# Splitting some projection products so that every four segment steps hold 3072 TensorE instructions

## The chip, the cores and the metric

The kernel runs on one core of a Trainium2 chip. The metric is the device time of one execution in microseconds (us). The kernel before took 1007.62 us, the median of three runs that lie between 1007.40 and 1008.14 us.

## The reference

Two blocks follow each other: a memory-augmented attention that walks through the sequence in segments of 32 rows, and a gated feed-forward block. The walk is a true recurrence: the memory rows that a segment returns are the memory rows of the next one.

```python
S, Dm, H, Dh, M, seg, F = 2048, 640, 32, 128, 8, 32, 1728
mem = mem0                                   # 8 rows
for s in range(S // seg):                    # 64 segments
    h = concat([mem, layernorm(x)[s * seg:(s + 1) * seg]])      # 40 rows x 640
    q, k, v = h @ Wq, h @ Wk, h @ Wv                            # 32 heads of 128
    p = softmax(where(mask, q @ k.T * Dh ** -0.5, -1e9))
    o = (p @ v) @ Wo                                            # 40 rows x 640
    mem = o[:M]
    outs.append(o[M:])
h = x + concat(outs)
out = h + (relu(layernorm(h) @ W_gate) * (layernorm(h) @ W_up)) @ W_down
```

## The kernel before

**Order of the work.** Every operation is recorded by hand, in program order, on its engine. A small dependency solver then adds the semaphore waits. Nothing is rescheduled: TensorE executes its instructions in the order in which the Python code adds them. A loop `for s in range(1, NSEG)` writes out the 63 segment steps after the first one, and the feed-forward block follows, four blocks of 512 rows. There is no loop left in the program; TensorE has one straight stream of about 48,800 instructions (a matmul that brings its own weight load counts as two, LDWEIGHTS and MATMUL).

**A projection on TensorE.** `project` multiplies the 640 columns of the segment's rows with one half (2048 columns) of Wk, Wq or Wv. The 640 contraction rows are five chunks of 128. In each chunk there are four products, one for each group `g` of 32 output partitions: the activations `act[:, c, :]` (128 x 32) are the stationary operand, 512 columns of the weights are the moving operand, and the result goes to partitions 32g to 32g+31 of a PSUM bank. So the 128 x 128 array is used as four column tiles of 32 columns, one for each `g`, and a projection of one half is 20 products of 512 columns. All four products of a chunk use the same activations, but each column tile has to load them for itself.

**Shared weight loads.** The function `again` (L359) emits a matmul without a LDWEIGHTS, for a column tile that still holds the right activations. In the loop of `WAYS`, the first half of a projection walks through the chunks 0 to 4 and the second half through 4 to 0. The second half therefore begins with the chunk that the first ended with, and with `held=True` its first four products go through `again`: four weight loads fewer. The value projection does the same after the query projection. That makes three places in a step, 12 weight loads, that are left out.

**A step on TensorE, in order:** keys, half 0 and half 1 (`project(a, ks, 1, ...)`, banks P2 and P3); the products of the probabilities with V of the step before (`pv_x`, L654); queries, half 0 and half 1 (banks P0 and P1); values of half 0, with the scores (L466) laid between; values of half 1, again with scores; then a denser tail: `pv_mem` (L519), `filler` parts, `wo_split` (L582, 32 products of 320 columns), `wo_pass` (L565, 64 products of 160 columns) and a last `filler(2)`. The memory rows of the next segment come out of L582 and L565 through `to_act_split` on VectorE (L605, L606), and the next step's key projection waits for them.

**What differs between steps.** The filler depends on `s % 4`. In steps with `s % 4` of 2, 3 and 0 it projects the memory rows of four later segments (`extra_units`, products of 512 columns on banks BQ). In steps with `s % 4 == 1` from s = 5 on it is `woe_pass` (L625, products of 320 columns with Wo), of which 28 products stand behind `wo_pass` as the last TensorE work of the step.

Of the kernel before, what the change touches and what calls it, by code (L numbers as in the profile page):

```python
# [163 lines left out]
def build_kernel(nc, A_x, A_mem0, A_Wq, A_Wk, A_Wv, A_Wo, A_seg_len, B_W_gate, B_W_up, B_W_down, out):  # L164
# [7 lines left out]
    DC = D // 128  # L172
# [91 lines left out]
    P0, P1, P2, P3 = 4, 5, 6, 7  # L264
# [97 lines left out]
            stop_tensor_calc=stop, tile_size=(128, 32 if g is not None else 128), tile_position=(0, 32 * (g or 0)),  # L362
            bass_skip_group_check=True, ldweights=False))

    def project(act, akeys, j, halves, banks, chunks=range(5), ends=(0, DC - 1), held=False):
        swap = 1 if j == 2 and akeys[0][0] == "acte" else 0

        def f(pe):
            for c in chunks:
                for n, i in enumerate(halves):  # L370
                    for g in range(4):
                        o = 2048 * i
                        w = (W[:, j, c, o + 512 * (g ^ swap):o + 512 * (g ^ swap) + 512] if j == 2 else
                             W[:, j, c, o:o + 2048].rearrange("p (h e) -> p h e", e=128)[:, :, 32 * g:32 * g + 32])
                        a = (bank(banks[n])[32 * g:32 * g + 32, :], act[:, c, :], w)
                        if n == 0 and not (held and c == chunks[0]):
                            ins = pe.matmul(*a, start=(c == ends[0]), stop=(c == ends[1]), skip_group_check=True)  # L377
                        else:
                            ins = again(pe, *a, c == ends[0], c == ends[1], g)
            return ins  # L380
        add("pe", f, r=list(akeys) + [("W", j, c) for c in chunks], w=[B(b) for b in banks] + [("Wdone", j)])
# [540 lines left out]
    row_stats(xl, ("xl",), n_rows(1))  # L922
    row_scale(xl, ("xl",), n_rows(1), xl, ("xl",))

    WAYS = ((range(DC),), (range(DC - 1, -1, -1), (DC - 1, 0), True))

    for s in range(1, NSEG):
        last = s == NSEG - 1
        par = s % 2
        nb = s // 4 + 1  # L930
        ln = 64 + 128 * nb < S

        e2 = EARLY.index((s + 1) // 4 * 4 - 1) if (s + 1) // 4 * 4 - 1 in EARLY else None
        e2c = EARLY.index(s - 4) if s - 4 in EARLY else None
        more = 64 + 128 * (nb + 1) < S
        units, evac = extra_units(s)
        woe = s % 4 == 1 and 5 <= s < NSEG - 3 or s == NSEG - 2

        def filler(n):
            if units:  # L940
                units(n)
            if woe:
                woe_pass(BQ[0], WPARTS[n])
        if s > 0:
            a, ks = pass_act(s)
            for i in range(2):
                project(a, ks, 1, (i,), ((P2, P3)[i],), *WAYS[i])
                to_tok((P2, P3)[i], i, "act")
                if last and i == 1:
                    load_piece(("Ko", 0), "act")  # L950
                flip(i, Ko, i, [("Ko", i)])
            if s % 4 == 2 and more:
                row_std(n_rows(nb + 1))
                row_scale(xl, ("xl",), n_rows(nb + 1), xl, ("xl",), "pool")
            if s % 4 == 1 and e2 is not None:
                row_std(128)
                row_scale(xt, ("xt",), 128, xt, ("xt",), "pool")
            pv_x(s - 1, 0)
            norm_x(0)
            if s % 4 == 0 and e2 is not None:  # L960
                add_attn(xt[:, :], xt, at, [("xt",), ("at",), ("rx",)], [("xt",)], "pool")
                dma(h_d[128 * e2:128 * e2 + 128, :], xt[:, :], r=[("xt",)], w=[("h_d", e2)])
            if s % 4 == 2:
                merge_v(s, 1)
            if not last:
                for i in range(2):
                    project(a, ks, 0, (i,), ((P0, P1)[i],), *WAYS[i])
                    to_tok((P0, P1)[i], 2 + i, "act")
                    flip(2 + i, Qo, i, [("Qo", i)])
                    if i == 0:  # L970
                        norm_x_late(0)
                        flip_ox(s - 1, (0,))
            else:
                norm_x_late(0)
                flip_ox(s - 1, (0,))
            if s == NSEG - 2:
                dma(xn2T[0][:, :, :], xn2_d[:, :, :], r=[("xn2_d", u) for u in range(4)] + [("Wdone", 0)],
                    w=[("xn2", 0, u) for u in range(4)])
            project(a, ks, 2, (0,), (P2,), range(4), held=not last)
            scores(s, 0, (0, 1))  # L980
            project(a, ks, 2, (0,), (P2,), (4,))
            scores(s, 0, (2, 3))
            if not last:
                exp_mem(s, 0)
                mask_mem(s, 0)
            to_v(P2, Vp, 0, ("Vp",), "act")
            if last:
                load_piece(("Vp", 0), "act")
            if s % 4 == 1 and ln:
                if n_rows(nb) == 128:  # L990
                    flip_rows(chunks_of(at[:, :]), xl, ("xl",), ("at",))
                else:
                    ln1_trans(nb, xl, ("xl",), BQ[1])
                if more:
                    ln1_load(nb + 1, xl, ("xl",))
        if last:
            project(a, ks, 2, (1,), (P3,))
            to_v(P3, Vp, 1, ("Vp",), "act")
            merge_v(s, 0)
            flip_ox(s - 1, (1,))  # L1000
            exp_x(s, 0)
            gate_up(0, 0)
            scores(s, 1)
            exp_x(s, 1)
            load_piece(("g1", 0), "act")
            mask_x(s)
            late_o(s - 1)
            break
        project(a, ks, 2, (1,), (P3,), range(4))
        scores(s, 1, (0, 1))  # L1010
        project(a, ks, 2, (1,), (P3,), (4,))
        scores(s, 1, (2, 3))
        flip_ox(s - 1, (1,))
        if s == NSEG - 2:
            load_piece(("Pm", 0))
        exp_mem(s, 1)
        to_v(P3, Vp, 1, ("Vp",), "act")
        merge_v(s, 0)
        pv_mem(s, 0)
        norm_mem(s, 0)  # L1020
        exp_x(s, 1)
        exp_x(s, 0)
        mask_mem(s, 1)
        flip_mem(s, 0)
        if e2c is not None:
            flip_rows(chunks_of(at[:, :]), xt, ("xt",), ("at",))
        filler(0)
        if s == NSEG - 2:
            load_piece(("om", 0))
        pv_mem(s, 1)  # L1030
        filler(1)
        norm_mem(s, 1)
        flip_mem(s, 1)
        late_q(s + 1, [("oT", par, "m", 1)])
        if s == NSEG - 2:
            p = 1 - place(s + 1)[0]
            add("pool", lambda o, p=p: o.tensor_copy(Qo[:, :, M:32], Qe[p][:, :, M:32]), r=[("Qe", p, i) for i in range(2)],
                w=[("Qo", i) for i in range(2)])
        if s > 0 and not woe and s != NSEG - 3:
            late_o(s - 1)  # L1040
        if s % 4 == 1 and ln:
            n = n_rows(nb)
            if n < 128:
                copy_op("act", chunks_of(at[:, :])[:, :, 0:n], chunks_of(bank_bf(BQ[1])[:, 0:D])[:, :, 0:n], [B(BQ[1])],
                        [("at",)])
            ln1_back(nb, chunks_of(at[:, :]), [("at",)], "pool")
        mask_x(s)
        if e2c is not None:
            dma(xn2_d[:, :, 128 * e2c:128 * e2c + 128], chunks_of(at[:, :]), r=[("at",)], w=[("xn2_d", e2c)])
        if s % 4 == 3 and e2 is not None:  # L1050
            dma(xt[:, :], x_ap[128 * e2:128 * e2 + 128, :], w=[("xt",)])
            load_attn(at, e2, [], ("at",))
        wo_split(par, P1)
        fold_split(P1, "dve" if s % 4 == 1 else "pool")
        wo_pass(par, P3, (1,))
        to_act_split(s + 1, P3)
        if s >= 1:
            rows_split(P3, P1, wtok, ("wtok",))
            store_attn(wtok, ("wtok",), M, 32 * (s - 1), RID)
        filler(2)  # L1060
        if woe:
            for n in ((s - 2, s - 1) if s == NSEG - 2 else (s - 1,)):
                late_o(n)
        if s % 4 == 0 and e2 is not None:
            row_moments(xt, ("xt",), 128)
        if s % 4 == 1 and more:
            row_moments(xl, ("xl",), n_rows(nb + 1))
        if evac:
            evac()
        if woe:  # L1070
            woe_sum(BQ[0])
            woe_store(s // 4 - 1)
        if s == NSEG - 4:
            p, j = place(NSEG - 1)
            add("pool", lambda o, p=p, j=j: o.tensor_copy(act_e[1 - p][:, :, M:32], act_r[p][:, j, :, M:32]),
                r=[("act", p, "x", j), ("act", p, "x")], w=[("acte", 1 - p)])
# [74 lines left out]
    s = NSEG - 1  # L1151
# [131 lines left out]
```

## Time and profile before

| what | value |
|---|---|
| median of three runs | 1007.62 us |
| the profiled execution's own time | 1006.39 us |
| its span from the first to the last instruction | 1004.7 us |
| TensorE busy | 971.1 us (97% of the span), 25153 matmuls |
| TensorE weight loads | 23308, beside the matmuls |
| VectorE, ScalarE, GpSimd busy | 712.9, 524.7, 167.4 us |
| granted TensorE clock | 1.000 |
| instruction transfers of queue q8 | 190 packets, 3.11 MB |

The profiled execution is 1.2 us shorter than the median of the other runs, and 1.7 us of its time lie outside the span. In the rows of groups, a line such as `L377 PE MATMUL ps<-W,act_r 128*32 128x512` names the source line, the engine, the operation, what is written and read, the array tile and the moving operand; behind the bar stand the busy time of the group and the mean duration of one in ns. The duration of a matmul is partly modelled; the distance between starts is what the stream costs. "Issue" as releaser means that the engine was idle and that the profile shows nothing that it waited for. A step of the loop takes about 12 us: the first key products of the steps 5 and 9 start at 105.28 and 153.91 us, 48.6 us for four steps.

### The profile page before, as it was taken

Reading aid. Unit: us, or ns where it says so; the run is one execution under the profiler, and the core shown is the slowest. Engines: PE = TensorE matmul, PEld = TensorE weight load, DVE = VectorE, ACT = ScalarE, POOL = GpSimd, SP = SyncE. Lnnn points to the kernel's source line nnn. Section 1 sums busy time; section 2 is a strip of 40 time slices with the busy share of each in tenths; the row PEclk is TensorE's granted clock in tenths of the full one; section 3 lists DMA queues with packets and bytes.
Section 4 is the critical chain, followed back from the end, with each engine's and each line's share of the span. In section 5 each row is a group of like instructions: output and inputs, shape, how many; then the busy total and the mean of one; then the engine's idle time right before and its main releaser. Section 6 shows DMA issues by size and latency. Waiting matters only on the chain.

```text
span 1004.7 us, 53813 instructions
## 1 busy us (share of the span) xinstructions
PE 971.1 (97%) x25153; PEld 495.7 (49%) x23308; DVE 712.9 (71%) x1863; ACT 524.7 (52%) x1331; POOL 167.4 (17%) x416
## 2 busy tenths in 40 slices
PE   3789999999999999999999999999999999999998
PEld 0245555555555554555555555555555555344443
DVE  2568787878878887888788878787878765445332
ACT  0456566556666666666666666665656643122121
POOL 7020202121302130222022212111110010000000
PEclk9999999999999999999999999999999999999999
DMA  9931212121212111121212131211111158413100
GB/s 373 418 102 28 53 28 55 33 55 50 53 41 54 49 53 47 47 54 47 53 41 63 47 55 40 41 41 38 40 29 40 38 165 251 108 20 92 27 14 26
DMA packets 72421, 73.01 MB, mean 73 GB/s; under 512 B 41632, under 2 KB 59008, under 8 KB 70272
## 3 DMA queue, kind: packets, MB, share of 16 engines
q1 hardware_dynamic: 70064, 68.27, 23.6%
q8 instruction: 190, 3.11, 1.3%
q10 hardware_dynamic: 2128, 1.31, 0.5%
q14 instruction: 39, 0.32, 0.1%
HBM read 37.04 MB, written 6.55 MB: 43 GB/s over the span
## 4 chain that ended last, share of the span: by engine, by line
PE 93%; SPq 3%; DMA 2%; issue 1%; DVE 1%; ACT 0%; POOL 0%; DVEq 0%; ACTq 0%
PE ps L377 43%; PE ps L841 11%; PE ps L359 10%; PE ps L565 7%; PE ps L582 6%; PE ps L625 4%; SPq L324 3%; PE ps L1088 3%; PE ps L466 2%; PE ps L654 2%; DMA Wo<-in_A_Wo_dram 2%; PE ps L519 2%; PE ps L854 0%; PE ps L1100 0%; DVE TBf L605 0%
## 5 line engine op out<-in xcount | busy, mean ns | idle before, releaser
L377 PE MATMUL ps<-W,act_r 128*32 128x512 bf16 x6832 | 447.4, 380 | 3.1 <-DVE act_r L606 1.8
L377 PEld LDWEIGHTS ps<-W,act_r 128*32 128x32 bf16 x6832 | 169.7, 96 | 212.0 <-issue 63.1
L401 ACT ACTIVATE tok<-ps 128x512 bf16<-128x512 f32 x190 | 109.3, 594 | 57.3 <-PE ps L377 48.8
L377 PE MATMUL ps<-W,act_e 128*32 128x512 bf16 x1224 | 120.0, 383 | 8.0 <-DMA W<-in_A_Wv_dram 3.7
L396 DVE STREAM_TRANSPOSE Ko<-tox 128x512 bf16<-128x512 bf16 x128 | 89.8, 703 | 42.7 <-ACT tox L401 41.5
L474 POOL COPY Qo<-Qe 128x256 bf16<-128x256 bf16 x64 | 28.0, 437 | 528.9 <-DVE oT L539 521.0
L401 ACT ACTIVATE tox<-ps 128x512 bf16<-128x512 f32 x134 | 79.6, 598 | 56.5 <-PE ps L377 35.5
L545 DVE STREAM_TRANSPOSE oT<-tox 128x512 bf16<-128x512 bf16 x128 | 89.8, 702 | 0.0
L396 DVE STREAM_TRANSPOSE Qo<-tok 128x512 bf16<-128x512 bf16 x124 | 85.6, 690 | 0.9
L565 PE MATMUL ps<-Wo,oT 128*32 128x160 bf16 x4032 | 82.3, 233 | 2.8 <-DMA Wo<-in_A_Wo_dram 1.7
L359 PE MATMUL ps<-W,act_e 128*32 128x512 bf16 x856 | 84.6, 385 | 0.0
L582 PE MATMUL ps<-Wo,oT 128*32 128x320 bf16 x2016 | 79.8, 299 | 0.5 <-DVE rm L529 0.5
L359 PE MATMUL ps<-W,act_r 128*32 128x512 bf16 x808 | 79.9, 382 | 0.0
L565 PEld LDWEIGHTS ps<-Wo,oT 128*32 128x32 bf16 x4032 | 71.8, 97 | 12.0 <-DMA Wo<-in_A_Wo_dram 2.8
L401 ACT ACTIVATE Vp<-ps 128x512 bf16<-128x512 f32 x127 | 75.2, 592 | 0.5 <-ACT Vp L401 0.5
L869 ACT ACTIVATE g<-ps 128x512 bf16<-128x512 f32 x52 | 30.1, 593 | 79.5 <-PE ps L841 79.5
L595 ACT ACTIVATE SA<-TA 64x40 f32<-64x40 f32 x126 | 29.5, 234 | 77.0 <-DVE TA L593 76.2
L841 PE MATMUL ps<-xn2T,Wu 128*128 128x512 bf16 x259 | 64.5, 379 | 0.1
L870 DVE TENSOR_TENSOR hT<-g,ps 128x512 bf16<-128x512 bf16 x52 | 35.7, 687 | 40.6 <-PE ps L841 38.6
L482 ACT ACTIVATE Pm<-ps 128x64 bf16<-128x64 f32 x126 | 28.1, 223 | 69.2 <-PE ps L466 69.2
L841 PE MATMUL ps<-xn2T,Wg 128*128 128x512 bf16 x247 | 61.8, 379 | 1.3 <-issue 1.0
L582 PEld LDWEIGHTS ps<-Wo,oT 128*32 128x32 bf16 x2016 | 53.9, 97 | 16.0 <-DVE rm L529 1.2
(116 smaller groups left out, 1463.1 us busy)
## 6 DMA issues: line engine op xcount, KB each, us to landing
VM<-Vp SPq DMA_DIRECT2D x126, 65.0 KB
VM<-Vp SPq DMA_DIRECT2D x63, 130.0 KB
W<-in_A_Wk_dram SPq DMA_DIRECT2D x5, 1024.0 KB
W<-in_A_Wq_dram SPq DMA_DIRECT2D x5, 1024.0 KB
W<-in_A_Wv_dram SPq DMA_DIRECT2D x5, 1024.0 KB
Wo<-in_A_Wo_dram SPq DMA_DIRECT2D x8, 640.0 KB
attn_d<-wtok SPq DMA_DIRECT2D x248, 7.5 KB
xt<-in_A_x_dram SPq DMA_DIRECT2D x16, 160.0 KB
```

The costliest lines, as they stand in the source:

```text
L324: add(eng, lambda e: e.dma_start(dst, src), r=r, w=w, dma=True)
L359: return pe.add_instruction(mybir.InstMatmult(name=nc.get_next_instruction_name(), engine=mybir.EngineType.PE, ins=[pe.lower_ap(rhs), pe.l ...
L377: ins = pe.matmul(*a, start=(c == ends[0]), stop=(c == ends[1]), skip_group_check=True)
L396: add("dve", lambda v: v.transpose(dst[:, 16 * i:16 * i + 16, 0:32], tok[t][:, :].rearrange("p (h f) -> p h f", f=32)), r=tok_keys(t), w=keys)
L401: add("act", lambda a: a.activation(dst, src, ACTF.Copy), r=r, w=w)
L545: add("dve", lambda v, kh=kh: v.transpose(ap(oT[p], 160 * kh + M, [[320, 4], [40, 4], [1, 32]]), ap(tox, 128 * kh, [[256, 4], [1, 4], [4, ...
L565: i = pe.matmul(bank(bk)[32 * gg:32 * gg + 32, 0:160], src[:, hb, 0:32], w[:, gg], start=(hb == CH[16 * halves[0]]), stop=(hb == CH[-1]), ...
L582: i = pe.matmul(bank(bk)[32 * q:32 * q + 32, 0:320], src[:, hb, 0:32], w, start=(n == 0), stop=(n == 7), skip_group_check=True)
L625: ins = pe.matmul(bank(bk)[32 * q:32 * q + 32, 0:320], src[:, hb, 0:32], w[:, 2 * (q % 2):2 * (q % 2) + 2], start=(i == 0), stop=(i == 15) ...
L841: ins = pe.matmul(bank(bk), w[:, c, lo:lo + 128], xn2T[par][:, c, :], start=(c == 0), stop=(c == DC - 1))
L870: add("dve", lambda v: v.tensor_tensor(hT[par][:, j, :], g1[gi][:, :], bank(bu), ALU.mult), r=[B(bu), ("g1", gi)], w=[("hT", par, j)])
L1088: i = pe.matmul(*a, start=(j == 0), stop=(j == FC - 1), skip_group_check=True)
```

## The change

`project` gets a parameter `parts`, the number of instructions to add in it. As long as some are left, a product (in a chunk that isn't the first one of the accumulation) is emitted as two of 256 columns, on the same column tile and PSUM bank, one after the other. With two or more left, the second one has its own LDWEIGHTS with the same activations (a split adds two instructions); with one left it goes through `again` (a split adds one). The order of products is otherwise unchanged: tile 0 first half, tile 0 second half, tile 1 first half, and so on.

`fill_of(s)` divides a number of instructions by step: 56, 39, 8 and 52 for `s % 4` of 0, 1, 2 and 3, with 26 in step 1, 29 in step 57 and none from step 61 on. First, up to three of the three `held` places get their four weight loads back (4 instructions each); the rest are splits in the key and query projections, shared over their four halves.

```diff
-    def project(act, akeys, j, halves, banks, chunks=range(5), ends=(0, DC - 1), held=False):
+    def project(act, akeys, j, halves, banks, chunks=range(5), ends=(0, DC - 1), held=False, parts=0):
...
+            left = parts
             for c in chunks:
                 for n, i in enumerate(halves):
                     for g in range(4):
...
                         if n == 0 and not (held and c == chunks[0]):
-                            ins = pe.matmul(*a, start=(c == ends[0]), stop=(c == ends[1]), skip_group_check=True)
+                            k = min(left, 2) if c != ends[0] else 0
+                            left -= k
+                            for q in range(2 if k else 1):
+                                b = a if not k else (a[0][:, 256 * q:256 * q + 256], a[1],
+                                                     w[:, 256 * q:256 * q + 256] if j == 2 else w[:, 8 * q:8 * q + 8])
+                                if q and k == 1:
+                                    ins = again(pe, *b, c == ends[0], c == ends[1], g)
+                                else:
+                                    ins = pe.matmul(*b, start=(c == ends[0]), stop=(c == ends[1]), skip_group_check=True)
                         else:
                             ins = again(pe, *a, c == ends[0], c == ends[1], g)
...
-    WAYS = ((range(DC),), (range(DC - 1, -1, -1), (DC - 1, 0), True))
+    WAYS = ((range(DC), (0, DC - 1)), (range(DC - 1, -1, -1), (DC - 1, 0)))
+    FILL = (56, 39, 8, 52)
+
+    def fill_of(s):
+        n = {1: 26, 57: 29, 61: 0, 62: 0, 63: 0}.get(s, FILL[s % 4])
+        alone = min(n // 4, 3)
+        rest = n - 4 * alone
+        return [k < 3 - alone for k in range(3)], [2 * ((rest // 2 + k) // 4) + (k == 0 and rest % 2) for k in range(4)]
...
+            held, parts = fill_of(s)
             for i in range(2):
-                project(a, ks, 1, (i,), ((P2, P3)[i],), *WAYS[i])
+                project(a, ks, 1, (i,), ((P2, P3)[i],), *WAYS[i], held=i == 1 and held[0], parts=parts[i])
...
-                    project(a, ks, 0, (i,), ((P0, P1)[i],), *WAYS[i])
+                    project(a, ks, 0, (i,), ((P0, P1)[i],), *WAYS[i], held=i == 1 and held[1], parts=parts[2 + i])
...
-            project(a, ks, 2, (0,), (P2,), range(4), held=not last)
+            project(a, ks, 2, (0,), (P2,), range(4), held=not last and held[2])
```

## The prediction

> **What bounds the kernel now.** I read the page from its busy times to the chain that ended last, then the TensorE timeline of some steps, and last the distances between starts, product by product.
>
> ```profile
> span 1004.7 us, 53813 instructions
> ...
> PE 971.1 (97%) x25153; PEld 495.7 (49%) x23308; DVE 712.9 (71%) x1863; ACT 524.7 (52%) x1331; POOL 167.4 (17%) x416
> ...
> q8 instruction: 190, 3.11, 1.3%
> ...
> PE 93%; SPq 3%; DMA 2%; issue 1%; DVE 1%; ACT 0%; POOL 0%; DVEq 0%; ACTq 0%
> ```
>
> TensorE's own stream carries 93% of the chain, so what the change adds or takes there goes into the time nearly one for one. The row q8 is TensorE's instructions on their way in: 3.11 MB over the 48,800 instructions of its stream are 64 bytes each, and 190 packets are 256 instructions each.
>
> The timeline of step 4's end gives the price of products on four column tiles:
>
> ```profile
> 102.13 1.26 PE L582 MATMUL ps<-Wo,oT 128*32 128x320 bf16 x32
> 103.22 1.28 PE L565 MATMUL ps<-Wo,oT 128*32 128x160 bf16 x64
> 104.33 0.39 PE L377 MATMUL ps<-W,act_e 128*32 128x512 bf16 x4
> 104.54 0.39 PE L359 MATMUL ps<-W,act_e 128*32 128x512 bf16 x4
> 104.76 0.39 PE L377 MATMUL ps<-W,act_e 128*32 128x512 bf16 x4
> ```
>
> From start to start, four products (one on each tile) of 512 columns take 0.216 us, of 320 columns 1.09 / 8 = 0.136 us, of 160 columns 1.11 / 16 = 0.069 us. Inside a group of four the starts are 1.7 to 4 ns apart. The tiles work side by side, and each is the length of its moving operand; L377 (with loads) and L359 (without) cost the same, as the loads run under the products before.
>
> What the change is aimed at is seen here:
>
> ```profile
> 115.34 1.07 PE L565 MATMUL ps<-Wo,oT 128*32 128x160 bf16 x51
> 116.65 0.45 PE L565 MATMUL ps<-Wo,oT 128*32 128x160 bf16 x13 [0.24 <-issue]
> ...
> 699.08 0.98 PE L625 MATMUL ps<-Wo,oTe 128*32 128x320 bf16 x21
> 700.71 0.45 PE L625 MATMUL ps<-Wo,oTe 128*32 128x320 bf16 x7 [0.65 <-issue]
> ...
> 807.93 0.31 PE L565 MATMUL ps<-Wo,oT 128*32 128x160 bf16 x6
> 809.06 1.21 PE L565 MATMUL ps<-Wo,oT 128*32 128x160 bf16 x58 [0.82 <-issue]
> ```
>
> TensorE stops in the middle of a run of equal products, and "issue" says that it waits for no semaphore. Counting instructions along the stream, the long stops of this kind stand at one place modulo 256 (193 to 195): the instructions 4547, 10435, 39619 and 46019, for instance, all 195. So they are ends of an instruction block. The q8 packets fit: after TensorE passes a block's end, a packet starts some 1.1 us later, takes 0.9 to 1.6 us, and where there is a stop it ends 1.2 to 1.5 us after the packet's end. From one end to the end of the next stop these are 3.4 to 4.6 us. Where 256 instructions last longer than that, nothing stops; all 512-column regions need over 4 us. Only dense tails stop. Over the steps, ten ends stop visibly, nine of them in steps with `s % 4 == 1` or in steps 32 and 52: about 5.0 us, plus 1.0 us in step 62.
>
> **Alignment.** Four steps have 2917 instructions before, so that ends drift through all places; after, 3072 = 12 x 256, so that they stand at the same twelve places in every cycle from step 3 to step 60. Counted in the changed stream the steps start at 201, 154, 152 and 153 modulo 256 (`s % 4` = 2, 3, 0, 1). With ends at 195 they lie, from a step's start, at 250 and 506; 41, 297, 553; 43, 299, 555; and 42, 298, 554, 810. Eleven are places without a stop in the trace (or close to one). The twelfth, 810 of 816 in `s % 4 == 1`, is three products before the end of L625. As the 39 added instructions stand earlier in the step, it is place 771 of 777 in the old count, and the block before it begins at 515, in L582. These 256 instructions (L582, L565, L625) last 3.28 us in the steps where nothing stops. The nearest ends in the trace are at 750, 756 and 764 (steps 13, 33, 53): all three stop, 0.60, 0.31 and 0.95 us, and TensorE resumes 3.89, 3.43 and 4.12 us after the end before. Against 3.28 us this leaves 0.61, 0.15 and 0.84, mean 0.53, of which 0.06 was spent anyhow waiting for act_r at the next step's first product (0.195 instead of 0.136 us there). So I put 0.47 us on each of the 14 steps 5 to 57: +6.6 us (ends: 0.1 x 14 = 1.4, 0.8 x 14 = 11). Gone are the 5.0 us of drifting stops; the 1.0 us of step 62 stays, for it has the same places but two instructions. Net +1.6 us (-3.6 to +6). The Trainium skill, "Runtime: NRT & Kernel Launch", section Instruction fetch mechanics, also has blocks of 256 instructions, but calls the fetch mostly hidden by the time that each instruction takes to dispatch; by that, alignment is worth 0. The trace disagrees in the tails, with 0.3 to 1 us a stop, and the trace decides.
>
> **Weight loads given back.** 165 places x 4 = 660 loads. A load has a row of 96 ns, but starts while the group of four before still streams (0.216 us); L377 and L359 have the same spacing. Cost 0. Without that cover, as in the first group behind a wait, the next group came 0.226 instead of 0.216 us later: 165 x 0.01 = 1.7 us is the most.
>
> **Splits.** The added matmuls are 828: 22, 14, 0 and 20 for `s % 4` = 0, 1, 2, 3 (15 x 22 + 15 x 20 + 7 + 13 x 14 + 9). A half of 256 columns lasts, between the rows of 160 and 320 columns, 69 + 67 x 96 / 160 = 109 ns. The columns are the same in sum. What counts is the order: both halves are on one tile, next to each other. The second must wait until the tile is free, 109 ns after the first. If later products, for other tiles, do not start ahead of a waiting one, tile 1's first half starts only there, 2 ns after, tile 2's another 111 ns on, and a fully split chunk lets the next one start after 4 x 111 = 444 ns instead of 216: 228 ns for four splits, 57 ns for one. The trace of before never puts two products on one tile in a row in these modes, so that it does not show which holds. It does show all starts in program order (line by line, through 23,900 products), and never a product that passes a waiting one; only weight loads start ahead. The bounds are: tiles go on independently, and a split costs a tile 2 x 69 - 136 = 2 ns, 828 x 2 / 4 = 0.4 us in all; or one behind the other, 828 x 57 ns = 47.2 us. I take the second. The Trainium skill, "TensorE: Matmul & The Clock Gate", Part 3, "The mechanism", speaks against the change in the same way: matmuls start and end in program order, strictly first in, first out; no run here shows it for two on one tile. These 47 us have no cover: no wait of TensorE stands in the key and query stages that could shrink, and the act_r wait stands at the chain's end.
>
> ScalarE and VectorE get the banks later by the same time and have nothing more to do. No DMA is added but nine instruction packets (2302 instructions). The clock is 1.000 and has no idle stretch to fall in.
>
> **Sum.** The profiled execution, 1006.4, + 47.2 + 1.6 + 0.4 (a quarter of the loads' bound) = 1055.6 us; against the median, which is 1.2 us higher, the same within what follows. Own range of this case: 1050 to 1064.
>
> **Rivals.**
> 1. *The tiles run on independently.* For it: the four tiles stream side by side, and weight loads do leave the order. Against it: no product was ever seen to do so. 1006.4 + 0.4 + 1.6 = 1008.4, with the alignment's bounds 1004 to 1013. A measurement of this kernel can tell about 0.2% (2 us) from no change, so this case holds all three signs.
> 2. *Faster: independent tiles and the end at 810 costs nothing.* This decides on the packet: if it lands early enough for TensorE to resume within 3.28 + 0.06 us of the end at 554, no stop is left but step 62's. Step 41 speaks for it: an end at 554, and at the next, 3.47 us later, no stop; step 45 needed less than 3.43. Against it stand steps 13, 33 and 53. 1006.4 + 0.4 - 5.0 = 1001.8 us.
> 3. *A split is dearer.* If the second half's load on the same tile is not hidden, each half pays the 10 ns of the fresh group above: 8 x 10 = 80 ns on a chunk, 20 ns a split, 16.6 us more: 1072 us. Against it: a load lasts 96 ns, a half 109.
>
> That the counts are not what the change says is no case: they are 3072 in the changed stream.
>
> **Chances.** Forecast 0.70; independent tiles 0.15; faster 0.06; dearer 0.09. Slower by over 0.2%: 0.70 + 0.09 + 0.06 of rival 1 = 0.85; within 0.2%: 0.06 of rival 1; faster 0.03 of it and 0.06 = 0.09. The forecast's case and the dearer one's lower end reach to 1066; taking in the upper half of rival 1 (0.09) needs 1007. That leaves out about 0.2.
>
> **What the profile after would show.** Matmuls near 25,981 and loads near 24,782, q8 at 199 packets; a group of 128x256 on the split's line. If the halves queue, the starts of a split chunk are about 0.11 us apart pairwise, and the key and query stages of steps with `s % 4` of 3, 0 and 1 are about 1.1, 1.25 and 0.8 us longer, while steps with `s % 4 == 2` keep 12.0 us: four steps take near 51.9 instead of 48.6 us. If these stages keep their length with the splits in, my forecast is wrong and rival 1 holds. Stops by "issue" should stand in L625 just ahead of the key projection of each step with `s % 4 == 2`, 0.1 to 0.8 us, and nowhere else until step 62; if they are missing there, the alignment pays and my term for it is wrong.

## The result and the profile after

The changed kernel took 1015.63 us (median of five runs), the kernel before 1007.35 us in the same comparison: a ratio of 1.0091 with a 95% interval of 1.0074 to 1.0108. A repeat gave 1.0088 (1.0073 to 1.0104). The change is slower by 9 us; the forecast was slower by 48 us.

A sixth execution of the changed kernel, the one profiled first, took 5677.59 us with its matmuls several times as long, at a granted clock of 1.000, and is left aside; "after" is the profile of the repeat, which took 1015.31 us. Its page:

```profile
span 1013.6 us, 56129 instructions
...
PE 975.6 (96%) x25995; PEld 539.8 (53%) x24782; DVE 716.0 (71%) x1863; ACT 524.7 (52%) x1331; POOL 167.5 (17%) x416
...
q8 instruction: 199, 3.26, 1.4%
```

The span is 8.9 us longer, but TensorE's busy time grew by 4.5 us only (971.1 to 975.6), although it has 828 matmuls more. (The rows differ by 842, because the trace of before lacks the records of 14 matmuls of the feed-forward block.) 199 instruction packets came in, nine more, as counted. The rest is time in which TensorE does nothing. First the query stage of step 4 (a step with 22 splits, 12 of them here), from the timeline:

```profile
97.11 0.42 PE L663 MATMUL ps<-VM,Px 64*32 64x129 bf16 x32
97.46 3.21 PE L386 MATMUL ps<-W,act_r 128*32 128x512 bf16 x68
100.50 0.19 PE L475 MATMUL ps<-Qo,Ko 128*32 128x40 bf16 x4
```

From the first `pv_x` product to the first score it takes 3.39 us with 68 matmuls: the 56 products that stood there before (40 of the queries, 16 of the values) and 12 second halves. Before, the same two starts lie 3.38 us apart:

```profile
95.49 0.42 PE L654 MATMUL ps<-VM,Px 64*32 64x129 bf16 x32
...
98.87 0.19 PE L466 MATMUL ps<-Qo,Ko 128*32 128x40 bf16 x4
```

The splits are nearly free. Now the end of step 53, from the timeline, to be laid beside the stop shown in the prediction at the same step:

```profile
704.68 1.30 PE L574 MATMUL ps<-Wo,oT 128*32 128x160 bf16 x64
705.79 1.00 PE L634 MATMUL ps<-Wo,oTe 128*32 128x320 bf16 x24
707.72 0.32 PE L634 MATMUL ps<-Wo,oTe 128*32 128x320 bf16 x4 [0.93 <-issue]
707.85 0.40 PE L386 MATMUL ps<-W,act_r 128*32 128x512 bf16 x4
```

L634 is the L625 of before. TensorE stops four products before the step's end; the key products behind it start at once when it goes on. And TensorE's waits in sum (line, releaser, us in total, times, longest):

```profile
PE ps L634 <- issue: 5.2, 9, 0.9
...
PE ps L574 <- issue: 1.9, 2, 1.1
```

Before (L565 is the L574 of the changed kernel):

```profile
PE ps L565 <- issue: 1.1, 2, 0.8
PE ps L625 <- issue: 1.0, 2, 0.7
```

This view only counts what lies beyond the modelled end of a matmul; from start to start the stops are longer. Measured so, 12 of the 14 steps with `s % 4 == 1` from 5 to 57 stop at instruction 809 of 816, for 0.25 to 1.09 us, 7.5 us in all. Only the steps 33 and 41 pass. The block ends among the key products, at the places 41 to 43 of a step, stop TensorE as well, in nine steps (3, 9, 11, 21, 23, 27, 40, 52, 57): from the first key product to the first `pv_x` product these take 0.09 to 0.40 us longer than the median of the steps with the same `s % 4`, 1.9 us in sum.

### The profile page after: what moved, and what is told of

It reads as the page before. It is cut to its first block, busy times and chain, and to the rows that moved or that the text cites. A ratio compares the mean times of both kernels' runs of the same rounds, so it can differ in the third digit from the quotient of the medians.

```text
span 5674.8 us, 56129 instructions
## 1 busy us (share of the span) xinstructions
PE 5657.5 (100%) x25995; PEld 1823.6 (32%) x24782; DVE 737.0 (13%) x1863; ACT 532.7 (9%) x1331; POOL 167.6 (3%) x416
## 4 chain that ended last, share of the span: by engine, by line
PE 100%; DMA 0%; DVE 0%; POOL 0%; ACTq 0%; issue 0%; POOLq 0%
PE ps L386 51%; PE ps L850 12%; PE ps L359 9%; PE ps L574 7%; PE ps L591 7%; PE ps L634 4%; PE ps L1105 3%; PE ps L475 2%; PE ps L663 2%; PE ps L528 1%; PE ps L863 0%; PE ps L887 0%; PE ps L1117 0%; DMA wtok<-in_A_mem_dram 0%; ACTq L324 0%
## 5 line engine op out<-in xcount | busy, mean ns | idle before, releaser
L386 PE MATMUL ps<-W,act_r 128*32 128x512 bf16 (+1 forms) x8306 | 2559.0, 1550 | 0.7 <-DVE act_r L615 0.7
L386 PEld LDWEIGHTS ps<-W,act_r 128*32 128x32 bf16 x8306 | 627.8, 291 | 1522.5 <-issue 1516.1
L386 PE MATMUL ps<-W,act_e 128*32 128x512 bf16 x1224 | 520.6, 1701 | 0.4 <-DVE TBf L456 0.4
L574 PE MATMUL ps<-Wo,oT 128*32 128x160 bf16 x4032 | 442.6, 798 | 0.0
L591 PE MATMUL ps<-Wo,oT 128*32 128x320 bf16 x2016 | 440.9, 1211 | 0.0
L574 PEld LDWEIGHTS ps<-Wo,oT 128*32 128x32 bf16 x4032 | 316.7, 321 | 158.2 <-issue 70.0
L359 PE MATMUL ps<-W,act_e 128*32 128x512 bf16 x856 | 365.9, 1708 | 0.0
L850 PE MATMUL ps<-xn2T,Wu 128*128 128x512 bf16 x260 | 364.0, 1708 | 0.0
L850 PE MATMUL ps<-xn2T,Wg 128*128 128x512 bf16 x260 | 361.3, 1698 | 0.0
L1105 PE MATMUL ps<-Wd,hT 128*128 128x320 bf16 (+1 forms) x225 | 259.6, 1197 | 0.0
L591 PEld LDWEIGHTS ps<-Wo,oT 128*32 128x32 bf16 x2016 | 162.8, 323 | 258.5 <-issue 248.6
L359 PE MATMUL ps<-Wd,hT 128*128 128x320 bf16 x195 | 236.2, 1211 | 0.0
L634 PE MATMUL ps<-Wo,oTe 128*32 128x320 bf16 x1024 | 228.7, 1214 | 0.0
L386 PEld LDWEIGHTS ps<-W,act_e 128*32 128x32 bf16 x1224 | 97.9, 319 | 297.9 <-issue 281.5
```

Of the source, the lines that this page charges most:

```text
L359: return pe.add_instruction(mybir.InstMatmult(name=nc.get_next_instruction_name(), engine=mybir.EngineType.PE, ins=[pe.lower_ap(rhs), pe.l ...
L386: ins = pe.matmul(*b, start=(c == ends[0]), stop=(c == ends[1]), skip_group_check=True)
L574: i = pe.matmul(bank(bk)[32 * gg:32 * gg + 32, 0:160], src[:, hb, 0:32], w[:, gg], start=(hb == CH[16 * halves[0]]), stop=(hb == CH[-1]), ...
L591: i = pe.matmul(bank(bk)[32 * q:32 * q + 32, 0:320], src[:, hb, 0:32], w, start=(n == 0), stop=(n == 7), skip_group_check=True)
L634: ins = pe.matmul(bank(bk)[32 * q:32 * q + 32, 0:320], src[:, hb, 0:32], w[:, 2 * (q % 2):2 * (q % 2) + 2], start=(i == 0), stop=(i == 15) ...
L850: ins = pe.matmul(bank(bk), w[:, c, lo:lo + 128], xn2T[par][:, c, :], start=(c == 0), stop=(c == DC - 1))
```

## The experiments

Theory A: the 9 us are stops at instruction block ends, which the alignment has put into the densest part of every fourth step. Theory B: the splits themselves cost it, at about 11 ns each instead of 57. Theory C: the weight loads given back cost it. Each ratio is taken against runs of the kernel before that stand beside it; its median in these groups lies between 1005.56 and 1007.35 us, so that times of different groups are best compared by their ratios.

**The changed kernel again**, unaltered.

> The changed kernel once more, unaltered, for a profile. Theory A (stops at block ends): the 9 us more are stops by 'issue' three products before the end of L625 in the steps with s % 4 == 1, from s = 5 to 57; 14 of them of about 0.5 to 1 us, 8 to 14 us in all against 5 us before, and the key and query stages keep their length. Theory B (price of splits): the stops are about as many us as before, and the key and query stages of steps with s % 4 of 3, 0 and 1 are each 0.1 to 0.25 us longer, 828 splits at about 11 ns. The prediction's own case (one half waits for the other, 57 ns a split) is out if those stages are less than 0.6 us longer. Time 1015 to 1018 us in every theory.

Measured: 1015.61 us, 1.0088 (1.0073 to 1.0104). From first key product to first key product, the median step with `s % 4` of 2, 3, 0 and 1 lasts 12.032, 12.045, 12.066 and 12.835 us (14 steps for the last); before, 12.049, 12.024, 12.027 and 12.217 us. So a step with 20 or 22 splits grew by 0.02 to 0.04 us, and the one with the stop by 0.6 us. Theory A expected 14 stops of 8 to 14 us in all; there are 12, of 7.5 us. Theory B expected the key and query stages 0.1 to 0.25 us longer; the query stage is 0.01 us longer. The prediction's own case would have added over 1 us to a step with 20 or 22 splits. The starts in two split chunks, in ns from the first key product of step 4, show why it did not ("whole" has 512 columns, "half" has 256):

```
whole, tiles 0 to 3:                       0, 3, 6, 10
eight halves, two on each tile:            226, 230, 233, 236; 335, 339, 342, 345
first half on tile 0; whole, tiles 1 to 3: 445; 448, 451, 455
second half on tile 0:                     554
whole, tiles 0 to 3 of the next chunk:     663; 664, 667, 670
```

In the third and fourth row, both halves of tile 0 stand ahead of the three whole products in the program. In the trace the second half starts 109 ns after the first, when its tile is free, and the three whole products start ahead of it. So the second half does wait, but it holds up its own tile alone: of the 154 chunks with halves and whole products, 147 show this order. In a chunk of eight halves the records don't name the tiles; read in the same way, the four first halves start together and the four second halves 109 ns later. Such a chunk takes 219 ns (226 to 445) instead of 216, 0.7 ns a split.

The timeline shows a product that passes another in step 57, where the split with one instruction left has its second half in L359. In the program nine products of L386 stand ahead of it, and the tenth, the whole product of tile 3, behind it. In the trace all ten start first:

```profile
743.99 0.61 PE L386 MATMUL ps<-W,act_r 128*32 128x512 bf16 x10
744.34 0.27 PE L359 MATMUL ps<-W,act_r 128*32 128x256 bf16 x1
```

**Block ends 20 instructions later.** The only edit is in step 1, far from the steps in question:

```diff
-        n = {1: 26, 57: 29, 61: 0, 62: 0, 63: 0}.get(s, FILL[s % 4])
+        n = {1: 6, 57: 29, 61: 0, 62: 0, 63: 0}.get(s, FILL[s % 4])
```

> The changed kernel with 6 instead of 26 instructions added in step 1, so that every later block end falls 20 instructions later in its step (830 of 816 instead of 810, that is 14 instructions into the next step; 574 instead of 554). The splits and loads of all other steps are the same. Theory A: the stops of the tails go, 1002 to 1006 us. Theory B: no change beyond 6 splits, 1015 to 1018 us.

Measured: 1013.38 us, 1.0071 (1.0059 to 1.0083). Theory A's number was a miss: the stops did not go, they moved 13 instructions into the next step:

```profile
PE ps L386 <- issue: 1.5, 4, 0.5
PE ps L574 <- issue: 1.3, 1, 1.3
```

They left the end of L634 and stand in the key products (L386): in 13 of the 14 steps these take, from the first one to the first `pv_x` product, 0.07 to 0.88 us longer than in step 58, which does not stop; 5.9 us in all. From `pv_x` to `pv_x` a step with `s % 4 == 1` has a median of 12.61 us here, 12.78 in the changed kernel and 12.19 in the shift by 60 below; the 0.42 us between the first and the last, in 14 steps, make the same 6 us, near the 0.66% (6.6 us) between the two ratios, 1.0071 and 1.0005. The 256 instructions before that place still last only 3.4 us. So 20 was too small a shift for A, and the run alone can't exclude B.

**Only the weight loads given back**, no split (`rest = 0`).

> Only the weight loads are given back, without a split; four steps have 2953 instructions and the block ends drift as before. Theories A and B: 1006 to 1010 us, like the kernel before, as loads hide under the products. Theory C (the loads given back are what costs): 1014 to 1017 us.

Measured: 1006.66 us, 1.0005 (0.9996 to 1.0014). Theory C falls: no cost of the loads can be told from zero.

**Only the splits**, with the loads shared (`return [True] * 3, ...`).

> Only the splits, with the weight loads shared as before; four steps have 3028 instructions and the block ends drift backwards by 44 in four steps. Theory A: the stops are those of a drifting order again, 1005 to 1010 us. Theory B: 1014 to 1017 us, as the splits are all there. The prediction's case would be 1050 us and more.

Measured: 1009.55 us, 1.0033 (1.0020 to 1.0046). All 828 splits are there, and two thirds of the 9 us are not. B is out as the main cause; for the 3 us see the run with all products split.

**Block ends 60 instructions later.** The steps from 4 to 60 are instruction for instruction those of the changed kernel; only where the blocks end in them differs.

```diff
-        n = {1: 26, 57: 29, 61: 0, 62: 0, 63: 0}.get(s, FILL[s % 4])
+        n = {1: 0, 2: 0, 3: 26, 57: 29, 61: 0, 62: 0, 63: 0}.get(s, FILL[s % 4])
```

> The changed kernel with no instruction added in steps 1 and 2 and 26 instead of 52 in step 3, so that every later block end falls 60 instructions later in its step than in the changed kernel: in steps with s % 4 == 1 at 102, 358 and 614, and then at 54 of the next step, among the key products. The steps from 4 to 60 have the same splits and loads and still 3072 instructions in four. Theory A (stops decide): 256 instructions that end at 54 hold 1.4 us of key products and last 3.7 us; no stop in steps 4 to 60 over 0.2 us, 1002 to 1005 us. Theory B (splits, loads or anything else in the added instructions): 1012 us and more, as after the shift by 20.

Measured: 1005.92 us, 1.0005 (0.9996 to 1.0013), about 1 us above theory A's range. The 9 us are gone with all splits and loads in place. The same end of step 53 on the timeline:

```profile
696.71 1.28 PE L574 MATMUL ps<-Wo,oT 128*32 128x160 bf16 x64
697.81 1.12 PE L634 MATMUL ps<-Wo,oTe 128*32 128x320 bf16 x28
698.83 1.26 PE L386 MATMUL ps<-W,act_r 128*32 128x512 bf16 x20
```

28 products run through, and in the waits one "issue" is left in the loop's tails, that of step 62:

```profile
PE ps L574 <- issue: 1.3, 1, 1.3
```

From the first `pv_x` product of step 2 to that of step 62 the trace has 728.8 us before, 735.2 in the changed kernel and 726.3 here: against before, the drifting stops are gone (-3.4 us) and the splits and the rest are paid (+0.9).

**The same with 109 instructions more in step 61**, to move the ends in step 62.

> As the shift by 60, with 109 instructions added in step 61, so that the ends in step 62 fall at 48, 304 and 560 and the next one at 38 of step 63, instead of 157, 413 and 669. Theory A: the stop of about 1 us in step 62's tail goes or shrinks, 0.5 to 1 us less than the shift by 60. Theory B: no gain, 0.1 to 0.6 us more for 48 splits.

Measured: 1004.78 us, 0.9989 (0.9979 to 1.0000), about 1 us under the shift by 60 alone. But the profile doesn't show the reason that A gave: step 62 stops 1.44 us in L591 and once more, 0.52 us, in the next key products, more than the 0.99 us of before. A packet comes late in that step: it starts 2.66 us after the block's end before here, 2.16 in the kernel before, 1.79 in the changed kernel and 2.60 in the shift by 20, while rows and weights of the feed-forward block are loaded (233 GB/s from 801 to 804.4 us, 54 from 790 to 795). What makes this version shorter is left open, and the interval reaches 1.

**All key and query products split**, 64 in a step, no alignment.

```diff
-        alone = min(n // 4, 3)
-        rest = n - 4 * alone
+        alone, rest = 0, 128 if n else 0
```

> All key and query products but those of each accumulation's first chunk are split, 64 in every step, with the weight loads shared as before; the count isn't aligned. The median length of steps with s % 4 of 2, 3 and 0 tells the price of a split apart from the stops. If a half waits for the other on its tile, a step is 3.6 us longer; if four products of any tiles start together, as the trace of the changed kernel has it, 0.06 to 0.15 us longer, 1 to 2.3 ns a split. The sum of stops grows, as 128 more instructions a step pass the ends; time 1010 to 1020 us.

Measured: 1040.9 us in one run, far over the 1020 that was expected. Yet the query stage with its 32 splits takes 3.404 us at the median, against 3.383 before: 0.66 ns a split. The shortest steps are 0.04 us longer, as 64 splits make. The medians with the stops in them, from `pv_x` to `pv_x`, are 0.3 to 0.9 us longer. The page:

```profile
span 1038.9 us, 61493 instructions
...
PE 990.2 (95%) x28993; PEld 625.0 (60%) x27148; DVE 714.5 (69%) x1863; ACT 524.7 (51%) x1331; POOL 167.7 (16%) x416
...
q8 instruction: 220, 3.60, 1.4%
```

Sixty steps hold 60 x 857 = 51,420 instructions, 201 blocks, and take 762.4 us: 3.8 us a block. By its products alone a block would have taken about 3.6 us by an estimate (the 728.8 us of before, less 3.4 of stops, with 2.5 for the splits, over 201), so this kernel waits for its instructions in many places: 86 of 199 blocks go on within 1.5 us of the end of their packet, as at the stops, against 23 of 178 in the changed kernel, 11 of 170 before and none of 179 in the shift by 60. Before, a block had 256 / 2917 of four steps, 4.26 us; after the change it has a twelfth, 4.05 us; with the splits only, 4.1 us. Added instructions are cheap on the array, but they leave a block less time. That the 3 us of the splits-only kernel come from here fits, but its profiled execution, at 1007.0 us, is the shortest of its five and shows no more stops than the kernel before, so it isn't shown.

**Two more places for the block ends**, 40 instructions earlier (step 1 gets 66), and 100 later (as the shift by 60, and step 4 gets 16 instead of 56).

> The changed kernel with 66 instead of 26 instructions added in step 1: every later block end falls 40 instructions earlier in its step, in steps with s % 4 == 1 at 514 and 770 instead of 554 and 810 (475 and 731 in the old count, where 256 instructions last 3.2 us without a stop). All else is as in the changed kernel. Theory A: the stops stay as long as they are at 810, 0.4 to 0.7 us in most of the 14 steps, but inside L625, 1013 to 1018 us. If only the seam between two steps matters, they go: 1003 to 1007 us.

Measured: 1011.98 us, 1.0050 (1.0033 to 1.0066).

```profile
PE ps L634 <- issue: 4.1, 6, 1.0
...
PE ps L591 <- issue: 1.4, 1, 1.4
```

The stops stay inside L634, in 6 of the 14 steps, 0.55 to 1.2 us. It isn't the seam between steps. In the six that stop, the next packet starts 1.34 to 1.63 us after TensorE passes the end before (at 514), in the eight that pass 0.29 to 1.00 us. There are fewer of them than A expected and the time is below its range.

> As the shift by 60, with 16 instead of 56 instructions added in step 4: ends 100 later than in the changed kernel, in steps with s % 4 == 1 at 398 and 654 and at 94 of the next step (359 and 615 in the old count, 3.25 us apart without a stop, and 4.25 us to the third). If the time of 256 instructions alone decides, stops of 0.3 to 0.6 us stand at 654 in 14 steps: 1009 to 1013 us. If it counts too that a packet is asked for earlier where the block before ends among long products, they are 0 to 0.15 us: 1003 to 1007 us.

Measured: 1005.76 us, 0.9985 (0.9976 to 0.9994): this version is faster than both kernels, by less than the 0.2% named in the prediction.

```profile
PE ps L574 <- issue: 1.7, 2, 1.2
```

One stop of 0.61 us in step 37, one of 0.16 us in step 29 and that of step 62 are all. The 256 instructions that end at 654 last 3.24 us without a stop, no longer than the 3.28 us of those that end at 810, and yet they hardly ever stop. So the time of the block isn't all: it matters when the packet that follows the end before it starts, and how long it takes. Here that end is at 398, among value products, and in 13 steps the packet starts between 0.25 us before and 1.04 us after TensorE passes it; in step 37 it starts 1.65 us after, and in step 29 it takes 1.49 us. In the changed kernel the end before is at 554, and the packet starts 1.23 to 1.42 us after it in the 12 steps that stop, 0.78 and 0.92 us in the two that pass. What sets the start of a packet isn't shown.

## Why the prediction was wrong

**The failed step is "Splits"**, and in it the choice between two bounds: "or one behind the other, 828 x 57 ns = 47.2 us. I take the second." That the second half waits until its tile is free, 109 ns after the first, was right. Its condition was wrong: "If later products, for other tiles, do not start ahead of a waiting one". They do, and so a tile loses only the 2 to 3 ns by which two halves are longer than a whole product. The price is about 0.7 ns a split (query stage 3.383 to 3.392 us with 12 splits, 3.404 with 32), so 828 of them cost 0.6 us, not 47.2. This is near the lower bound that stood in the prediction (0.4 us), and the mechanism of rival 1 held. I took the far end for two reasons. One was that no product had been seen to pass a waiting one; but in the kernel before the four tiles run in step with equal products, so that none with a free tile stood behind a waiting one, and the trace said nothing either way. The other was the Trainium skill, "TensorE: Matmul & The Clock Gate", Part 3, "The mechanism", by which matmuls start strictly in program order. This case's trace disagrees: in chunks of halves and whole products the whole ones start about 0.1 us ahead of a half that stands before them. Rival 3 falls too, as a chunk of eight halves takes 3 ns more and not 80.

Rival 1's time did not hold: 1008.4 us, 1004 to 1013 with its bounds, against 1015.3 in the profiled execution. Of the 6.9 us between them, 0.9 lie at the twelfth end, 1.6 in the drifting stops, which were 3.4 and not 5.0 us, 1.9 at ends among the key products, 1.2 in step 1 and 1.2 behind step 62; the next two paragraphs give these numbers. So its term for the alignment, +1.6 us, was mis-sized.

**The alignment was right in kind and in its worst place, and too small in size.** The twelfth end stops, at the place counted (810, measured 809), in L634. The prediction put 6.6 us on its 14 steps; measured are 7.5 us. But of the eleven ends of which it said "Eleven are places without a stop in the trace (or close to one)", three stop too, those at 41 to 43, in nine steps and for 1.9 us. The 256 instructions before them last 3.78 to 3.99 us without a stop; in seven of the nine steps the packet took 1.32 to 1.64 us, and in the steps 27 and 57 it started 1.66 and 1.88 us after the end before. The resume times it took from the steps 13, 33 and 53 (3.89, 3.43, 4.12 us) are borne out by 3.28 to 4.39 us, mean 3.82, over the 14. The stops of before were 3.4 us by the same count (the time beyond streaming at block ends, steps 2 to 61); the prediction's 5.0 us had counted the groups beside them too. Not counted was an end in step 1's tail. In the loop the alignment cost 7.5 + 1.9 - 3.4 = 6.0 us, at the upper end of the prediction's -3.6 to +6.

The 8.9 us of span lie so: 0.1 ahead of step 1's `pv_x`; 1.2 from step 1's to step 2's (12.07 before, 13.27 after); 6.5 from step 2's to step 62's; 1.2 behind that, of which only so much is known that the block ends moved there as well. Of the 6.5, the stops at 809 less those of before make 7.5 - 3.4 = 4.1, the ends among the key products 1.9 and the splits 0.6, which is 6.6. In the shift by 60 no key stage is more than 0.01 us longer than the median of its kind.

**Weight loads:** nothing that can be told from 0, as predicted (1.0005, 0.9996 to 1.0014). **"The clock is 1.000":** so it is in the repeat's profile.

**Rival 2** was wrong for this kernel, right for others: with the ends of the blocks elsewhere the drifting stops go and none take their place, and the steps 2 to 62 take 726.3 instead of 728.8 us with the splits in them. The whole does not come down to rival 2's 1001.8 us; the lowest median is 1004.78.

The Trainium skill, "Runtime: NRT & Kernel Launch", section Instruction fetch mechanics, has the block size right (the stops are 256 apart); that the fetch is mostly hidden by dispatch time is contradicted by 7.5 us of stops here, and by a kernel that ran at 3.8 us a block.

## What to carry to other kernels

A price for which the trace has no row should not be taken from an order of starts alone: where a mechanism has never been exercised in the trace, "never seen to happen" is no evidence, and the near bound deserved as much weight as the far one. And when a trace is read afterwards, go by what each record says it is (here its number of columns), not by the order that the program would give. In a long unrolled stream, count instructions per microsecond: where 256 of them lasted less than about 4 us, a block end could stop the engine here, and moving the count by 60 far upstream was worth 0.8%. Aligning a loop with the blocks makes its best and its worst place permanent, so choose the place by the time of the block by how early the packet at the end before it starts, and by trying more than one.

## What the runs showed of the hardware

- Of two matmuls of 256 columns on the same 32-column tile, next to each other in the stream, the second starts 109 ns after the first. Matmuls behind it in the stream, for other tiles, start ahead of it, 3 to 4 ns apart. Eight halves on four tiles take 219 ns, four whole products 216.
- After a block's end in the dense tail, a packet of 16 KB starts 0.8 to 1.4 us later, takes 0.9 to 1.6 us, and TensorE resumes 1.1 to 1.5 us after its end where it has to wait. For 14 ends at the same place this made 3.28 to 4.39 us. The two that did not stop had the earliest starts (0.78 and 0.92 us) and short packets (0.90 and 0.88 us).
- With 128 instructions more a step, whose products alone would need about 3.6 us a block, TensorE ran at 3.8 us a block: 33.6 us more over sixty steps, of which the splits' own price is 2.5 us.
